# Q/K, V and FFN up projections as two 64-row array tiles, with the last FFN weights placed in dead attention weights

## The chip, the cores and the metric

The kernel runs on one core of a Trainium2 chip. The metric is the device time of one execution in microseconds (us). Executions of one kernel on one chip agree within about 0.3% of their median (seven of the kernel before: 3549.8 to 3565.8 us). Experiments 1 to 11 are one run each, and for a single run the state is listed as unknown. Each experiment was run beside the kernel before on the same chip, and that time is given with it: 3553, 3561 or 3572 us. Where runs of two chips are compared directly, a difference is uncertain by up to these 18 us.

## The reference, cut to what matters

Two layers of a recurrent attention and a SwiGLU FFN, applied one after the other to 2048 rows of width D = 576. Attention takes 64 segments of 32 rows; each has 8 memory rows in front, which are the output of the segment before, so the segments run in order.

```python
for s in range(n_seg):                      # 64 segments of 32 rows
    h = concat([mem, x[s]])                 # 40 rows x 576
    q, k, v = h @ Wq, h @ Wk, h @ Wv        # 32 heads of 128
    p = softmax(mask(q @ k.T * scale))
    o = (p @ v) @ Wo
    mem = o[:8]                             # next segment waits for this
x = x + attention(layernorm(x))
x = x + (silu(n @ w1) * (n @ w3)) @ w2      # n = layernorm(x), F = 4608
# ... and the same again (second layer, same weights)
```

## The kernel before

Layer 2 follows layer 1 by 8 segments, so there are 72 steps: 8 with layer 1 alone, 56 with both (80 columns: 2 x 40 rows), 8 with layer 2 alone. FFN work is placed between the attention stages of the steps. A scheduler orders the instructions of each engine at build time; the order then stands.

TensorE writes to 8 PSUM banks. Scores, PV and the output have four; attention's projections and the FFN share the other four in two rings:

```python
accA = Ring(banks[4:6])     # Q, K, V, transposes
accB = Ring(banks[6:8])     # FFN
...
def s_qk(gi):               # a group of 4 or 6 heads
    for kind in range(2):                       # Q, then K
        acc = accA.take()                       # one bank each
        for hl in range(hg):
            for c in range(4):                  # D = 4 x 128 + 64
                mm(accv[:, hl], lhsT=Wm[:, c, ...], rhs=ht_cols(c), ...)
            mm(accv[:, hl], lhsT=T1[...], rhs=ht_cols(tailc), ...)  # zero-padded to 128 rows
        nc.scalar.activation(QKT[...], acc[...], ACT.Copy)          # Q is copied out while K runs
def s_v(gi):                # pieces of 512 and 256 columns, one bank each
    for pi, (a0, a1) in enumerate(pieces):
        acc = accA.take()
        ...                                     # 5 matmuls
        evac("act" if pi == 0 else "dve", VG[...], acc[...])
```

576 rows of contraction make 4.5 chunks of 128; the kernel pays for 5.

## Time and profile before

| | before |
|---|---|
| median of 2 runs | 3557.41 us |
| TensorE busy | 93% |
| granted TensorE clock, mean | 0.984 |
| matmuls | 58470 |
| changes of array mode in the build order | 1437 |
| end of first step, step with both layers, tail after the last step | 79.9, 49.7 (mean), 78.3 us |

"Mode" is the shape of the array that a matmul uses: all of it, or tiles of it. The page of the profile and the timeline lines are shown in the prediction.

### The profile page before, as it was taken

To read this page: it belongs to the slowest core of one execution; us is meant where nothing else is said; L and a number is where in the kernel's file an instruction comes from. 1 tells how busy PE (TensorE), PEld (TensorE's weight loads), DVE (VectorE), ACT (ScalarE), POOL (GpSimd) and SP (SyncE) were. 2 spreads that over 40 slices of the span, in tenths; PEclk is the share of its full clock that TensorE was granted. 3 is DMA by queue.
4 is the path that set the end of the run, shared out by engine and by line. 5 is a ranking of instruction groups with operands and counts; after the bars stand their busy time and mean duration, and the time that the engine had idled before them with its cause. 6 is when DMAs were issued, how large, how long until landed. Compare 5 with 4: busy or idle time off the path is not lost.

```text
span 3562.8 us, 131473 instructions
## 1 busy us (share of the span) xinstructions
PE 3323.7 (93%) x58470; PEld 2801.4 (79%) x58470; DVE 1916.3 (54%) x5614; ACT 1621.3 (46%) x3865; POOL 61.8 (2%) x109
## 2 busy tenths in 40 slices
PE   5999999999999999999999999999999999999996
PEld 4888877877787778878787878878787878888785
DVE  3455555555555555555555555555555555555553
ACT  2544544444444444444444444444444444444441
POOL 1000000000000000000000000000000000000000
PEclk8999999999999999999999999999999999999997
DMA  8033323223222322323222322323222323223236
GB/s 256 3 95 89 102 82 95 76 73 102 74 84 69 97 87 82 89 74 96 76 82 72 101 86 82 88 74 96 77 84 73 102 77 92 83 71 96 78 114 183
DMA packets 504617, 321.65 MB, mean 90 GB/s; under 512 B 31081, under 2 KB 501361, under 8 KB 504049
## 3 DMA queue, kind: packets, MB, share of 16 engines
q1 hardware_dynamic: 500976, 306.17, 29.5%
q8 instruction: 458, 7.50, 0.9%
q0 software_dynamic: 3072, 7.08, 0.6%
q14 instruction: 111, 0.90, 0.1%
HBM read 308.42 MB, written 2.36 MB: 87 GB/s over the span
## 4 chain that ended last, share of the span: by engine, by line
PE 64%; issue 18%; DMA 8%; DVE 6%; ACT 2%; POOL 1%; SPq 0%; POOLq 0%; DVEq 0%; ACTq 0%
PE bank L174 62%; DMA W13M<-in_B_w_dram 7%; PE bank L177 2%; POOL LNS L239 1%; DVE TT L534 1%; DVE XR L491 1%; DMA T<-in_A_Wq_dram 1%; DVE LNS L233 1%; DVE LNS L234 1%; DVE HTT L535 1%; DVE XN L240 1%; DVE XR L548 0%; DVE PB L405 0%; DVE STAT L402 0%; ACT TT L533 0%
## 5 line engine op out<-in xcount | busy, mean ns | idle before, releaser
L174 PE MATMUL bank<-HT,T 128*128 128x80 bf16 x4608 | 847.0, 204 | 3.9 <-DVE HT L276 3.9
L174 PE MATMUL bank<-XTB,W13M 128*128 128x256 bf16 (+1 forms) x5184 | 695.6, 263 | 88.7 <-DMA W13M<-in_B_w_dram 80.2
L174 PE MATMUL bank<-WV,HT 128*104 128x512 bf16 (+1 forms) x2880 | 629.7, 341 | 1.7 <-ACT QKT L355 1.0
L355 ACT ACTIVATE QKT<-bank 128x480 bf16<-128x480 f32 (+1 forms) x864 | 452.2, 524 | 374.2 <-PE bank L174 325.8
L533 ACT ACTIVATE TT<-bank 128x256 bf16<-128x256 f32 (+1 forms) x648 | 233.6, 360 | 826.5 <-PE bank L174 826.3
L174 PEld LDWEIGHTS <-W13M 128*128 128x128 bf16 x5184 | 450.9, 99 | 172.7 <-DMA W13M<-in_B_w_dram 107.3
L174 PEld LDWEIGHTS <-HT 128*104 128x104 bf16 x3600 | 411.3, 128 | 191.4 <-DMA T<-in_A_Wv_dram 14.7
L174 PE MATMUL bank<-HT,WQ 128*128 128x80 bf16 x9216 | 494.5, 204 | 41.1 <-ACT HT L471 22.2
L174 PE MATMUL bank<-OT,WO 128*128 128x80 bf16 x11520 | 516.1, 202 | 12.3 <-ACT OT L429 12.1
L174 PEld LDWEIGHTS <-WO 128*128 128x128 bf16 x11520 | 473.6, 100 | 43.0 <-issue 14.2
L174 PEld LDWEIGHTS <-WQ 128*128 128x128 bf16 x9216 | 439.8, 101 | 65.5 <-issue 46.2
L174 PE MATMUL bank<-HT,WK 128*128 128x80 bf16 x9216 | 484.8, 204 | 1.4 <-DVE HT L278 1.2
L174 PEld LDWEIGHTS <-T 128*128 128x128 bf16 x4608 | 466.4, 101 | 0.6
L174 PEld LDWEIGHTS <-WK 128*128 128x128 bf16 x9216 | 437.6, 101 | 3.1 <-DVE HT L278 2.1
L534 DVE SCALAR_TENSOR_TENSOR TT<-TT,bank 128x256 bf16<-128x256 bf16 (+1 forms) x648 | 250.7, 387 | 348.3 <-ACT TT L533 346.0
L174 PE MATMUL bank<-W2C,HTT 128*128 128x288 bf16 x2284 | 349.2, 288 | 18.1 <-DVE HTT L535 10.7
L395 DVE TENSOR_TENSOR SME<-bank,maskb 104x240 f32<-104x240 f32 (+1 forms) x432 | 162.3, 376 | 351.1 <-PE bank L174 350.3
L183 DVE CAST VG<-bank 104x256 bf16<-104x256 f32 x288 | 122.1, 424 | 424.4 <-ACT VG L181 225.9
L174 PE MATMUL bank<-XTB,W13T 128*128 128x256 bf16 (+1 forms) x1296 | 338.3, 263 | 0.0
L181 ACT ACTIVATE VG<-bank 104x512 bf16<-104x512 f32 x432 | 257.7, 597 | 169.1 <-PE bank L174 160.5
L548 DVE SCALAR_TENSOR_TENSOR XR<-bank,XR 128x288 f32<-128x288 f32 x576 | 259.3, 455 | 112.1 <-PE bank L174 105.5
L174 PEld LDWEIGHTS <-HTT 128*128 128x128 bf16 x2304 | 215.0, 98 | 83.4 <-issue 20.0
(67 smaller groups left out, 3400.9 us busy)
## 6 DMA issues: line engine op xcount, KB each, us to landing
W13M<-in_B_w_dram SPq DMA_DIRECT2D x648, 256.0 KB, 3.0
W2C<-in_B_w_dram SPq DMA_DIRECT2D x319, 288.0 KB, 3.2
W13T<-in_B_w_dram SPq DMA_DIRECT2D x648, 32.0 KB, 2.6
XR<-in_A_x_dram POOLq DMA_DIRECT2D x16, 288.0 KB, 4.8
WO<-in_A_Wo_dram SPq DMA_DIRECT2D x1, 4608.0 KB, 20.6
WQ<-in_A_Wq_dram SPq DMA_DIRECT2D x4, 768.0 KB, 9.8
WK<-in_A_Wk_dram SPq DMA_DIRECT2D x4, 768.0 KB, 12.9
WV<-in_A_Wv_dram SPq DMA_DIRECT2D x4, 768.0 KB, 13.7
```

What stands on the lines that cost most here:

```text
L174: return _chain(nc.tensor.matmul(*a, **k))
L177: return _chain(nc.tensor.transpose(*a, **k))
L181: nc.scalar.activation(out_ap, in_ap, ACT.Copy)
L183: nc.vector.tensor_copy(out_ap, in_ap)
L233: nc.vector.bn_stats(st[:, 0, :], X[:, 0:288])
L234: nc.vector.bn_stats(st[:, 1, :], X[:, 288:576])
L239: nc.gpsimd.tensor_tensor(rstd, ve, mhalf[:], op=ALU.pow)
L355: nc.scalar.activation(QKT[:, qs, kind, 0:hg, :], acc[:, 0:hg * 2 * QW].rearrange("p (b n) -> p b n", b=hg), ACT.Copy)
L395: nc.vector.tensor_tensor(sme, Sps[0:104, 0:hg, :], maskb[0:104, :].unsqueeze(1).to_broadcast([104, hg, QW]), op=ALU.add)
L533: nc.scalar.activation(tt, GAv, ACT.Tanh, scale=0.5)
L534: nc.vector.scalar_tensor_tensor(tt, tt, 1.0, GAv, op0=ALU.add, op1=ALU.mult)
L548: nc.vector.scalar_tensor_tensor(Xs, yp[:, 0:288], 0.5, Xs, op0=ALU.mult, op1=ALU.add)
```

## The change

The intent: chunks of 64 rows, nine of them, two at a time side by side. Q runs on rows 0 to 63 of the array and K on rows 64 to 127; likewise the two halves of V, and w1 with w3. Nine pairs should cost 4.5 passes in place of 5. Each pair writes two PSUM banks, so a stage takes two banks at once. The other parts: matmuls of one-layer steps use only the 40 columns in use; FFN down is done per two blocks, not four; the last FFN job's weights are loaded into attention weights that are no longer needed.

```diff
-    WQ = wp.tile([P, 4, H * E], BF, name="WQ")
-    WK = wp.tile([P, 4, H * E], BF, name="WK")
...
+    WQK = wp.tile([P, NCH, H * E], BF, name="WQK")        # NCH = 9; rows 0-63 Wq, 64-127 Wk
+    WV = wp.tile([P, NCH, H * E // 2], BF, name="WV")
...
         def s_qk(gi):
-            for kind in range(2):
-                acc = accA.take()
...
+            accs = [accA.take(), accA.take()]
+            for hl in range(hg):
+                for c in range(NCH):
+                    for kind, r in ((0, 0), (1, R64)):
+                        mm(views[kind][:, hl, q0:q1], lhsT=WQK[r:r + R64, c, ...],
+                           rhs=ht_cols(r, POS[c]), ..., tile_position=(r, 0))
             for kind in range(2):
+                nc.scalar.activation(QKT[...], views[kind][:, :, q0:q1], ACT.Copy)
         def s_v(gi):
+            accs = [accA.take(), accA.take()]              # two halves of 384 or 256 columns
...
+        def up():                                           # FFN, two blocks of 128
+            if last:
+                w13, state["w2"] = tail_w[pr]               # already in WQK, WV, WO
...
+            accs = [accB.take(), accB.take()]               # gate, up
```

## The prediction

> **What bounds the kernel now.** I read the page first: busy shares, then the chain that ended last, then the groups.
>
> ```profile
> PE 3323.7 (93%) x58470; PEld 2801.4 (79%) x58470; DVE 1916.3 (54%) x5614; ACT 1621.3 (46%) x3865; POOL 61.8 (2%) x109
> ...
> PE 64%; issue 18%; DMA 8%; DVE 6%; ACT 2%; POOL 1%; SPq 0%; POOLq 0%; DVEq 0%; ACTq 0%
> PE bank L174 62%; DMA W13M<-in_B_w_dram 7%; PE bank L177 2%; POOL LNS L239 1%; DVE TT L534 1%; DVE XR L491 1%; DMA T<-in_A_Wq_dram 1%; DVE LNS L233 1%; DVE LNS L234 1%; DVE HTT L535 1%; DVE XN L240 1%; DVE XR L548 0%; DVE PB L405 0%; DVE STAT L402 0%; ACT TT L533 0%
> ...
> L174 PE MATMUL bank<-HT,T 128*128 128x80 bf16 x4608 | 847.0, 204 | 3.9 <-DVE HT L276 3.9
> L174 PE MATMUL bank<-XTB,W13M 128*128 128x256 bf16 (+1 forms) x5184 | 695.6, 263 | 88.7 <-DMA W13M<-in_B_w_dram 80.2
> ```
>
> TensorE is busy 93% of the span and holds the chain; DVE and ACT have room. A weight transfer holds 7% of the chain. But a matmul's 204 ns is latency, not what it costs in a stream. The cost is the distance from one start to the next, which the timeline shows at 1704 us (a two-layer step):
>
> ```profile
> 1704.14 0.32 PE L174 MATMUL bank<-HT,WQ 128*128 128x80 bf16 x4
> 1704.29 0.20 PE L174 MATMUL bank<-HT,T 128*128 128x80 bf16 x1
> 1704.33 0.31 PE L174 MATMUL bank<-HT,WQ 128*128 128x80 bf16 x4
> 1704.47 0.20 PE L174 MATMUL bank<-HT,T 128*128 128x80 bf16 x1
> 1704.51 0.31 PE L174 MATMUL bank<-HT,WQ 128*128 128x80 bf16 x4
> ```
>
> One head of Q is five matmuls in 0.18 us: 36 ns each for 80 columns. The same view gives 109 ns for 256 columns, 217 for 512, 122 for 288: time goes with columns, 0.417 ns each plus 2.5, and weight loads hide. With these, the before kernel's 58470 matmuls come to: Q/K 826, V 623, FFN up 631, WO 413, FFN down 282, PV 83, scores and their transposes 120, other transposes 52, together **3030 us**.
>
> Two further lines show what a change of array shape costs and what tiles side by side can do:
>
> ```profile
> 1703.49 0.27 PE L174 MATMUL bank<-XTB,W13T 128*128 128x256 bf16 x1
> 1703.69 0.23 PEld L174 LDWEIGHTS <-QKT 128*64 128x64 bf16 x11 [0.21 <-issue]
> 1703.69 0.33 PE L174 MATMUL bank<-QKT 128*64 128x40 bf16 x11
> ...
> 152.63 0.36 PE L174 MATMUL bank<-QKT 128*64 128x40 bf16 x6
> ```
>
> From the last full-array start to the first 64-column start is 0.20 us where streaming explains 0.11: some 0.09 us of drain, which recurs both ways (start distances at all changes without another wait have a median of 93 ns over the stream). The build order of the before kernel has 1437 such changes: 134 us. The other lines: 11 scores alternating between two column tiles start 14 ns apart ((0.33 - 0.19) / 10), while 6 on one tile (one layer only) start 34 ns apart ((0.36 - 0.19) / 5). So two tiles do run at once, and instructions can be issued at least every 14 ns.
>
> 3030 + 134 = 3164 of 3563 us; the remaining 400 us are waits. The step boundaries (the YTS copies) lie about 32 us apart while only one layer runs, 41 to 45 with one layer and FFN, and 50 in the 56 two-layer steps. By my count a two-layer step needs 46 us of matmuls and drains, so it waits 4.
>
> **What the Trainium skill says.** "TensorEngine Tiling (Array Packing)", Key Properties: tiles load and multiply independently, and "Changing tiling mode (not just tile) drains the TensorE". The trace agrees on both for column tiles (14 against 34 ns; 93 ns). It holds no stream of row tiles. The same page, Gotcha 1: row tiles must not write one PSUM bank at the same time; hence the change holds two banks per stage. "TensorE: Matmul & The Clock Gate", The mechanism: matmuls start strictly in order, so a run of matmuls on one tile is not paired with a later run on the other. No line here shows that for rows.
>
> **The change, part by part.**
> 1. *Fewer columns.* D = 576 is 4.5 chunks of 128, and before paid 5; nine 64-row chunks, two at once, pay 4.5. If every pair ran as one: Q/K 16128 pairs of 80 columns at 36 ns and 4608 of 40 (one-layer steps, now trimmed) at 25 = 695 us (-131); V 2592 x 162.5 + 1296 x 109 = 563 (-60); up 4536 x 109 + 1296 x 56 = 568 (-63); WO and PV trimmed in the one-layer steps, at an estimated 25 ns, -33. Sum **-287**.
> 2. *Broken pairs.* In the changed kernel's build order the scheduler does not keep pairs: runs such as 17 matmuls on rows 0-63 and then 17 on rows 64-127. Matching neighbours greedily leaves 8109 Q/K, 1266 V and 2071 up matmuls alone. Each pays a whole slot for half the work: 114 + 94 + 89 = +297; small differences in transposes add 5. So the stream comes to 3044 against 3030: **+15**. The column saving is given back.
> 3. *Drains.* Now Q/K, V and up are in 64-row mode and WO, PV and down in full mode, and the scheduler mixes them: 3145 mode changes, not 1437. At 93 ns, 292 against 134: +159. I count two thirds, because many sit where PE waits anyway (my choice): **+106**.
> 4. *Weight transfers.* Two whole up-weight slots in place of three halves let the next 256 columns load early. PE lost 80 us to W13M by the group above, part of it in the tail; I take **-60**.
> 5. *Tail.* After the last step, FFN weights stream at 185 GB/s while PE is half idle:
>
> ```profile
> 3484.00:3563.00 79.00, 47.46 (x443) 36.73 (x443) 28.66 (x98) 11.71 (x39) 1.14 (x2) 0.76 0.62 185
> ```
>
>    The last job needs 15.9 MB. Its loads can now begin once the last Q/K is done, some 17 us before the last step ends, at up to the 285 GB/s of the start: 15.9 / 285 = 56 us, plus norm and store. I take **-20**.
> 6. *Banks.* Q and K end together and both banks must be copied out (ACT, 524 ns each) before V, which takes both too. Before, one bank drained while the other filled. The two copies plus latency are about 1.3 us; PV, WO and FFN work fill much of it. 432 groups at about 0.12 us left over: **+50**. FFN down copies out twice as often (DVE 455 ns x 576 more = 262 us), merged FFN ops give some back: DVE goes to about 60%, no bound.
>
> Sum: 3557 + 15 + 106 - 60 - 20 + 50 = **3648**.
>
> **Rivals.** (a) *64-row to full is no drain.* Only the 573 changes among the other shapes then cost: 53 us against 134, two thirds of which is -54 in place of +106: 3488. For it: only column-mode changes are measured here; against it: the skill's sentence covers all modes. (b) *Row tiles do not overlap*: each matmul would pay its own slot, 41472 Q/K matmuls alone cost about 1390 us, and the kernel needs over 4500. The column tiles speak against it; I give it 2%. (c) *PSUM copies become the bound of the step*: at 0.5 us per group and stage not 0.12, 432 x 0.76 us more gives 3900+. ACT at 46% and DVE at 54% speak against; part of it may come. (d) *Everything pairs and waits were what PE lost most*: stream 2750, giving about 3300. The build order speaks against it, unless hardware pairs more than neighbours.
>
> **Range and chances.** I weigh the sum (3648) 0.5, rival (a) (3488) 0.45, and (d) 0.05: about 3559, and with a little for (c) **3570**. Each branch is uncertain by some 90 us (waits of 1.5 us a step are 84 us over 56 steps), so 8 in 10 lie in **3390 to 3710**. Over 2% faster is below 3486, over 2% slower above 3629: rival (a) splits about evenly between faster and same, the sum leans to slower. Chances **0.30 / 0.38 / 0.32**.
>
> **What would show it.** Pairing: two Q/K starts of opposite rows within 14 ns, the next pair 36 ns on. Broken pairs: runs on one tile still 36 ns apart. Drains: full to 64-row start distances 0.09 us over streaming, and PEld idle put down to issue grown well above before's 192 us. Transfers: waits for W13 nearly gone. Tail: span after the last YTS copy about 58, not 78 us. Banks: PE waiting for the Q/K and V copies, which now is under 15 us. One-layer steps should fall from 32 to about 27 us, two-layer steps stay at 48 to 52. The prediction fails low if mode changes cost nothing or pairs re-form, high if bank waits pass 0.3 us a group.

## More of the kernel before

One more stretch of the timeline of before will be compared later (columns: start, duration, engine, line, operation, operands, count). It is the end of a Q/K group and the start of V.

```profile
1705.13 0.44 ACT L355 ACTIVATE QKT<-bank 128x320 bf16<-128x320 f32 x1
...
1705.55 0.20 PE L174 MATMUL bank<-HT,T 128*128 128x80 bf16 x1
...
1705.58 0.38 PE L174 MATMUL bank<-PTS,VG 104*128 104x80 bf16 x6
...
1705.80 1.04 PE L174 MATMUL bank<-WV,HT 128*104 128x512 bf16 x4
...
1706.14 0.42 ACT L355 ACTIVATE QKT<-bank 128x320 bf16<-128x320 f32 x1
```

Q was copied out of its bank at 1705.13, while K still ran. K ends, six small PV matmuls follow, and V starts at 1705.80 in Q's old bank. K's copy comes only at 1706.14: V did not need to wait for it.

## The result, and the profile after

| | before | after |
|---|---|---|
| median of 2 runs | 3557.41 us | **4125.26 us** |
| ratio | | 1.1595 (95%: 1.1561 to 1.1628) |
| TensorE busy | 93% | 89% |
| granted clock, mean | 0.984 | 0.961 |
| matmuls; mode changes | 58470; 1437 | 86197; 3145 |
| end of first step; step with both layers; tail | 79.9; 49.7; 78.3 us | 96.5; 58.3; 79.1 us |

A ratio here is the mean time of one kernel's fast runs over that of the other's fast runs of the same rounds, so it is not quite the ratio of the medians. The changed kernel is 16% slower, far outside the predicted range of 3390 to 3710.

The page of the changed kernel (busy shares, then the chain by engine, then groups with the idle time before them and what ended most of it):

```profile
PE 3677.9 (89%) x86197; PEld 3032.9 (74%) x86197; DVE 2198.5 (53%) x5575; ACT 1473.8 (36%) x3631; POOL 63.3 (2%) x109
...
issue 55%; PE 25%; DVE 11%; ACT 4%; DMA 2%; SPq 2%; POOL 1%; DVEq 0%; POOLq 0%; ACTq 0%
...
L169 PE MATMUL bank<-WV,HT 64*104 64x384 bf16 (+1 forms) x7776 | 813.9, 325 | 114.4 <-ACT QKT L345 111.7
L169 PEld LDWEIGHTS <-HT 64*104 64x104 bf16 x7776 | 606.1, 129 | 233.2 <-issue 163.4
```

No engine became the bound: TensorE, DVE and ACT all have a smaller busy share than before. V's matmuls now have 114 us of idle time ahead of them, nearly all ended by ACT's QKT copy; before it was 1.7 us. "Issue" is time for which the profile names no releaser, drains among it. In the view of waits, weight loads (PEld) before and after:

```profile
PEld L174 <- issue: 192.4, 625, 4.1
```

```profile
PEld L169 <- issue: 628.8, 1783, 6.6
```

And the stretch of the timeline of after that answers to the one shown of before:

```profile
2010.65 0.53 PE L169 MATMUL bank<-HT,WQK 64*128 64x80 bf16 x5
...
2011.16 1.03 ACT L345 ACTIVATE QKT<-bank 128x480 bf16<-128x480 f32 x2 [3.21 <-PE bank L169]
2011.78 1.90 PE L169 MATMUL bank<-WV,HT 64*104 64x384 bf16 x9 [0.60 <-ACT QKT L345]
```

Q and K end together. ACT then copies both banks, one after the other, for 1.03 us. V stands for 0.60 us until the first copy frees a bank, and the second half of V needs the second copy. (The clock was granted at half in this stretch and in full in the one of before, so the durations of matmuls are not to be compared.)

To see where all the time went I took the start times of all TensorE matmuls from each trace, in the build order, and split each distance to the next start: column time (columns x 0.417 ns + 2.5 ns, with some slack, twice that where the clock was granted at half) is stream; at a mode change up to 0.1 us beyond it is drain; the rest is wait. The sums, in us:

| | before | after | after, four shared banks | after, emission order | after, both |
|---|---|---|---|---|---|
| stream | 3111 | 3243 | 3006 | 3046 | 2912 |
| of the stream, added by half clock | 40 | 142 | 109 | 184 | 102 |
| drain | 136 | 300 | 244 | 222 | 219 |
| wait | 301 | 566 | 321 | 1072 | 508 |
| mode changes | 1437 | 3145 | 2597 | 2335 | 2335 |
| matmuls without a neighbour on the other rows | - | 11446 | 4524 | 0 | 0 |
| clock at half (records of the trace) | 116 | 325 | 247 | 455 | 272 |

So of the 562 us that the span grew, stream is +132, drain +164 and wait +265. Half clock explains 102 of the 132: where it was granted, Q/K matmuls of 80 columns start 67 ns apart in place of 36. At full clock the stream grew by 30 only. The drain is an upper bound, because the split counts 0.1 us at a change before it counts any wait: 730 of the 3145 changes (73 us of drain) lead into a further wait of over 0.02 us, which may hide it; before, 156 of 1437 (16 us). Without these, drain grew by 106. The last three columns are experiments below.

### The profile page after: what moved, and what is told of

Same layout as the page of the kernel before. It is cut to its first block, busy times and chain, and to the rows that moved or that the text cites. A ratio compares the mean times of both kernels' runs of the same rounds, so it can differ in the third digit from the quotient of the medians.

```text
span 4124.6 us, 185858 instructions
## 1 busy us (share of the span) xinstructions
PE 3677.9 (89%) x86197; PEld 3032.9 (74%) x86197; DVE 2198.5 (53%) x5575; ACT 1473.8 (36%) x3631; POOL 63.3 (2%) x109
## 4 chain that ended last, share of the span: by engine, by line
issue 55%; PE 25%; DVE 11%; ACT 4%; DMA 2%; SPq 2%; POOL 1%; DVEq 0%; POOLq 0%; ACTq 0%
PE bank L169 25%; SPq L207 2%; DMA W<-in_B_w_dram 1%; DVE HTT L525 1%; ACT QKT L345 1%; DVE SME L372 1%; ACT SME L377 1%; DVE SME L376 1%; DVE STAT L375 1%; DVE XR L476 1%; DVE HTT L526 1%; DVE XR L539 1%; POOL LNS L232 1%; PE bank L172 1%; DVE STAT L379 1%
## 5 line engine op out<-in xcount | busy, mean ns | idle before, releaser
L169 PEld LDWEIGHTS <-WQK 64*128 64x128 bf16 x42048 | 955.0, 97 | 167.9 <-issue 133.3
L169 PE MATMUL bank<-HT,WQK 64*128 64x80 bf16 (+1 forms) x41472 | 1006.6, 196 | 69.1 <-ACT HT L455 16.4
L169 PE MATMUL bank<-WV,HT 64*104 64x384 bf16 (+1 forms) x7776 | 813.9, 325 | 114.4 <-ACT QKT L345 111.7
L169 PEld LDWEIGHTS <-HT 64*104 64x104 bf16 x7776 | 606.1, 129 | 233.2 <-issue 163.4
L169 PE MATMUL bank<-XTB,W 64*128 64x256 bf16 (+1 forms) x11016 | 750.9, 261 | 28.1 <-DVE XR L539 18.6
L169 PEld LDWEIGHTS <-W 64*128 64x128 bf16 x11016 | 561.4, 94 | 125.7 <-issue 32.1
L178 DVE CAST VG<-bank 104x384 bf16<-104x384 f32 (+1 forms) x432 | 221.0, 512 | 743.1 <-PE bank L169 731.5
L169 PE MATMUL bank<-OT,WO 128*128 128x80 bf16 (+1 forms) x11520 | 538.6, 197 | 27.3 <-ACT OT L406 22.1
L539 DVE SCALAR_TENSOR_TENSOR XR<-bank,XR 128x288 f32<-128x288 f32 x1152 | 498.1, 453 | 119.5 <-PE bank L169 89.7
L169 PE MATMUL bank<-W2C,HTT 128*128 128x288 bf16 x2232 | 433.9, 287 | 80.2 <-DVE HTT L525 36.0
L345 ACT ACTIVATE QKT<-bank 128x480 bf16<-128x480 f32 (+3 forms) x864 | 374.7, 482 | 284.8 <-PE bank L169 279.6
```

The costliest lines, as they stand in the source:

```text
L169: return _chain(nc.tensor.matmul(*a, **k))
L178: nc.vector.tensor_copy(out_ap, in_ap)
L345: nc.scalar.activation(QKT[:, qs, kind, 0:hg, q0:q1], views[kind][:, :, q0:q1], ACT.Copy)
L539: nc.vector.scalar_tensor_tensor(Xs, yp[:, 0:288], 0.5, Xs, op0=ALU.mult, op1=ALU.add)
```

## The experiments

**Theory**: the stage that holds both of accA's banks is the root. V needs two banks, and its halves can run side by side only once both are copied out. TensorE waits, and the scheduler, which estimates when banks come free, breaks the pairs (one half starts in the bank that is free first) and puts other modes' work between. **Rivals**: the mode changes alone; the broken pairs alone; row tiles that overlap poorly.

One number is used throughout: the distance from the last Q/K start of a group to the next V start, and the column time of other matmuls placed in it. What is left over is uncovered; it holds the waits and the drains of this stretch (after: about 0.56 and 0.18 us; after with four shared banks: 0.05 and 0.14).

| mean over about 430 to 450 groups, us | other work | distance | uncovered |
|---|---|---|---|
| before | 0.50 | 0.57 | 0.07 |
| after | 0.73 | 1.43 | 0.70 |
| before, holding two banks | 0.68 | 1.06 | 0.38 |
| after, emission order | 0.51 | 1.36 | 0.85 |
| after, four shared banks | 0.48 | 0.66 | 0.18 |

**1. What a change between the full array and 64 rows costs.** The tail matmul of V in the kernel before has zeros in half its rows; here it is issued on the other 64 alone.

```diff
-                    mm(acc[0:104, 0:a1 - a0], lhsT=HTt[:, 4, :], rhs=T2[:, a0:a1], start=False, stop=True)
+                    mm(acc[0:104, 0:a1 - a0], lhsT=HTt[0:64, 4, :], rhs=T2[0:64, a0:a1], start=False, stop=True,
+                       tile_position=(0, 0))
```

> The kernel before, with only the fifth matmul of each V piece issued on 64 rows (the zero half of its operands left out); nothing else is changed, and its build order differs in 61 places of 58470. Mode changes go from 1437 to 2809, 1372 more. If a change between the full array and 64 rows drains as the column-mode changes of before do (about 96 ns): +132 us, some 3690. If it is no drain (rival a of the prediction): 3557 within 0.5%.

Measured: 3708.34 against 3571.94, +136 us for 1372 more changes, 99 ns each. The timeline of this run shows single ones:

```profile
1812.29 1.04 PE L174 MATMUL bank<-WV,HT 128*104 128x512 bf16 x4
1813.26 0.42 PE L174 MATMUL bank<-T,HT 64*104 64x512 bf16 x1
1813.69 0.60 PE L174 MATMUL bank<-WV,HT 128*104 128x256 bf16 x4
1814.21 0.31 PE L174 MATMUL bank<-T,HT 64*104 64x256 bf16 x1
```

From 1813.69, four matmuls of 256 columns should take 0.44 us; the 64-row one starts after 0.52. The way back (1813.26 to 1813.69, one matmul of 512 columns at 0.217) costs 0.21 more here; in 422 of 430 such places of this trace it is 0.13. Rival (a) of the prediction, that these changes are free, falls. At 99 ns, the 1708 changes that the change added are worth at most 170 us; how much of that is hidden in waits no run shows.

**2. Holding two banks, with nothing else of the change.** In the kernel before, Q and K are interleaved by head and both copied at the end; the V pieces likewise. Full array throughout.

```diff
-            for kind in range(2):
-                acc = accA.take()
+            accs = [accA.take(), accA.take()]
+            for hl in range(hg):
+                for kind in range(2):
...
+            for kind in range(2):
+                acc = accs[kind]
                 nc.scalar.activation(QKT[:, qs, kind, 0:hg, :], ...)
```

> The kernel before, all on the full array, but Q and K of a group are interleaved by head and both PSUM banks are held until both are done, and the two V pieces likewise, as the changed kernel holds them. Mode changes 1326, not more than before. If holding both banks is a main cause: waits for the QKT and VG copies rise by over 100 us, time 3650 to 3800. If the mode changes and broken pairs are the cause and banks are covered by other work: under 3600.

Measured: 3719.31 against 3571.94, +147 us, with fewer mode changes than before (1326) and 720 more matmuls, since V of a four-head group is split in two here. Uncovered time per group went from 0.07 to 0.38 us; 0.31 x 432 is 134 of the 147 us. By the split, wait rose by 151, stream by 13, and drain fell by 10. Holding two banks costs time without any row tile.

**3. The pairs kept together.** The changed kernel with TensorE in emission order.

```diff
-    FORCE_PE_ORDER=False,
+    FORCE_PE_ORDER=True,
```

> The changed kernel with all TensorE instructions kept in the order in which the program emits them: all 30456 pairs stand side by side (24733 with 5670 or more matmuls left single in the changed kernel, 11446 single in all), and mode changes fall from 3145 to 2335. If broken pairs and mode mixing are the main cause: minus about 250 us of stream and 78 us of drains, some 3800. If the reordering mostly used time in which TensorE would have waited for a bank anyway: 4100 or above, with waits for the copies up by what the stream lost.

Measured: 4358.36 against 3571.94 of before. All pairs stand, stream falls by 197 us and drain by 78, as hoped; waits rise by 506. So the broken pairs and mixed modes are not the root: the scheduler spent them to fill time in which TensorE would have waited for banks, and it gained by that.

**4. Four banks for attention and FFN together.** The only edit is the ring:

```diff
-    accB = Ring(banks[6:8])
+    accA.slots = list(banks[4:8])
+    accB = accA
```

> The changed kernel with one ring of four PSUM banks for attention and FFN in place of two rings of two, so that Q/K and V need not wait for each other's copies unless FFN took the banks between. In its build order mode changes fall to 2597, single matmuls from 11446 to 4524. If bank holding is the root (it breaks pairs and makes the scheduler mix modes): 3700 to 3850. If row tiles simply overlap poorly: within 2% of 4125.

Measured: **3588.85** against 3571.94, below the range that was expected if banks were the root. Of the 16%, all but 0.5% is gone by that one edit: 536 us. (Before gains by the same edit too; see the control.) Stream fell by 237, drain by 56, wait by 245. The timeline of this run at a Q/K group's end:

```profile
1809.42 0.85 PE L170 MATMUL bank<-HT,WQK 64*128 64x80 bf16 x38
...
1810.20 0.39 PE L170 MATMUL bank<-PTS,VG 104*128 104x80 bf16 x6
1810.36 1.03 ACT L346 ACTIVATE QKT<-bank 128x480 bf16<-128x480 f32 x2 [0.91 <-PE bank L170]
...
1810.52 1.62 PE L170 MATMUL bank<-WV,HT 64*104 64x384 bf16 x14
```

ACT copies for 1.03 us as before, but V starts 0.16 us after the copies begin, in two other banks.

**5. The control: the same ring in the kernel before.**

```diff
-    accB = Ring(banks[6:8])
+    accA.slots = list(banks[4:8])
+    accB = accA
```

> The kernel before with the one ring of four PSUM banks, as the control of the changed kernel's run with it. If the shared ring took 536 us off the changed kernel because only that one holds two banks per stage, before gains little: 3480 to 3560, from waits of 100 us at most for banks and from 1240 mode changes in place of 1437 (19 us). If four shared banks are simply better for any such kernel: under 3350.

Measured: 3474.56 against 3553.45, -79 us (2.2%), 5 us below the expected range. The ring helps before too: its uncovered time per group does not move (0.07), but its waits shrink by 64 us in all, some 20 each at FFN down and at Q/K. So 457 of the 536 us belong to what the change did with the banks. With four shared banks in both kernels, the change still costs 114 us (about 96 when each is taken against before on its own chip), although it contains the trimming of one-layer steps, which experiment 10 finds worth 80.

**6. Emission order with four banks.** The edits of experiments 3 and 4 together.

```diff
-    FORCE_PE_ORDER=False,
+    FORCE_PE_ORDER=True,
...
-    accB = Ring(banks[6:8])
+    accA.slots = list(banks[4:8])
+    accB = accA
```

> The changed kernel with the shared ring of four banks and with TensorE kept in emission order: all pairs side by side, 2335 mode changes (2597 without the pin). With two rings of two banks the pin cost 233 us (4358 against 4125). If that was banks alone, it now costs under 100 us or even gains: 3500 to 3690. If the scheduler's filling of other waits (softmax, FFN) is what counts: 3750 or more.

Measured: 3657.05 against 3553.45. The pin costs 68 us in place of 233. Against experiment 3 this is also the cleanest test of the banks: the 86197 matmuls run in the same order, with the same pairs and the same 2335 changes, and only the ring differs. It takes 701 us off (4358 to 3657), 564 of them wait. TensorE's wait for the Q/K copies, in experiment 3 and here (total, times, longest):

```profile
PE bank L169 <- ACT QKT L345: 257.0, 367, 2.7
```

```profile
PE bank L170 <- ACT QKT L346: 32.4, 26, 2.9
```

The stream, all in pairs, is 2912 us. At full clock, two Q/K starts of opposite rows are most often 3 or 4 ns apart, and a pair of 80 columns takes 36 ns (median), just what one full-array matmul took; pairs of 256 and 384 columns take 109 and 163. Row tiles overlap fully. But waits, for which no filling is left, are 187 us above those of the free order.

**7. A faster copy, which was not faster.** DVE copies K's bank while ACT copies Q's.

```diff
-                nc.scalar.activation(QKT[:, qs, kind, 0:hg, q0:q1], views[kind][:, :, q0:q1], ACT.Copy)
+                evac("act" if kind == 0 else "dve", QKT[:, qs, kind, 0:hg, q0:q1], views[kind][:, :, q0:q1])
```

> The changed kernel with K's bank copied out by DVE while ACT copies Q's, so that both banks of accA come free some 0.5 us earlier in each of 432 groups; 3145 mode changes as before, single V matmuls 787 in place of 1266. If the time until both banks are copied is what V waits for: 0.2 to 0.5 us a group, 90 to 210 us less, 3915 to 4035. If the waits have another cause, or DVE's queue is no faster: 4080 or more.

Measured: 4270.97 against 3561.34 of before; 146 us slower than the changed kernel, where I had expected 90 to 210 faster. In the trace the first copy ends 0.64 us after the last Q/K matmul in both kernels (medians), but the second ends 1.49 us after it on the mean, not 1.16. That DVE was still in other work then is the likely reason, and not shown. From first to last start, V takes 1.83 us in place of 1.57 on the mean. By the split, wait rises by 95 us (by 107 ahead of V) and half clock adds 67 (489 us granted at half, not 327), while the stream is otherwise 19 shorter. My expectation of the sign was wrong, because I took DVE for free at 53% busy. The later bank fits the theory, but nearly half of the loss is clock.

**8. Attention and FFN apart.** The FFN as before (full array, one bank a block, no tail load), attention in row tiles on two banks.

```diff
-            accs = [accB.take(), accB.take()]
+                acc = accB.take()
...
-                        mm(v[:, fb, lo:hi], lhsT=w13[r:r + R64, c, ...], rhs=XTB[r:r + R64, POS[c], lo:hi], ...,
-                           tile_position=(r, 0))
+                        mm(accv[:, gu, lo:hi], lhsT=W13M[:, wss[gu], c, ...], rhs=XTB[:, c, lo:hi], ...)
```

> The changed kernel with the FFN as in the kernel before (full array, one bank a block, four blocks to a down step, no tail load); attention still in row tiles on two banks. To compare with the changed kernel without tail load (4144). If the loss lies in the attention's banks: 3950 or more. If the FFN's two-bank units and their mode changes (3159 to 2675, 48 us) carry as much: 3750 to 3850.

Measured: 3963.77, as expected if most of the loss lies in attention's banks. Against the changed kernel without tail load (next), 180 us go with the FFN's part of the change; the other 402 us over before (3561.34 on this chip) remain with attention's part alone.

**9. Without the tail load.**

```diff
-        last = 4 * j + 4 >= NSEG + LAG
+        last = False
```

> The changed kernel with the last job's FFN weights loaded through the rings as in all other jobs. The tail after the last YTS copy is 79 us in both kernels. If loading into the dead attention weights gained what the slower landing in 64 partitions costs: tail above 85 us and time above 4130. If it gave nothing: 4125 within 10 us.

Measured: 4144.12 (before on this chip: 3553.45), against 4125.26: the tail load is worth 19 us. The tail after the last step is 101.8 us without it and 79.1 with it; before it was 78.3, and 80.2 in experiment 8, with the FFN of before. So it only wins back what the new FFN lost. The issue view points to one likely reason: before, an up transfer of 128 partitions, and after, one of 64 partitions (columns: size, median us from issue to landing). Half clock and other differences of the two FFNs were not separated from it.

```profile
W13M<-in_B_w_dram SPq DMA_DIRECT2D x648, 256.0 KB, 3.0
```

```profile
W<-in_B_w_dram SPq DMA_DIRECT2D x612, 288.0 KB, 4.8
```

And the tail of after, in the same columns as the prediction's line for before (busy times, then clock, DMA share and GB/s at the end): 154 GB/s, where before reached 185.

```profile
4045.50:4124.60 79.10, 66.56 (x730) 56.78 (x730) 33.33 (x80) 8.76 (x21) 1.14 (x2) 0.65 0.74 154
```

**10. Trimmed one-layer steps and four banks, full array.** Of the change, only the 40-column matmuls in one-layer steps are put into the kernel before, with the shared ring.

```diff
+        q0, q1 = layers[0] * QW, (layers[-1] + 1) * QW
...
-                mm(PVv[:, hl, :], ..., rhs=PTS[0:104, ss, hl, :],
+                mm(PVv[:, hl, q0:q1], ..., rhs=PTS[0:104, ss, hl, q0:q1],
```

Q/K, WO and the copies after them are cut to q0:q1 in the same way.

> The kernel before with the shared ring and with the changed kernel's trimming of the one-layer steps (Q/K, PV and WO on 40 columns where only one layer runs), the full array everywhere. Trimming takes 5120 Q/K and 2560 WO and 512 PV matmuls from 36 to about 25 ns: 90 us off the run with the shared ring alone, if those steps are bound by TensorE; 40 us or less if their copies and softmax bind them.

Measured: 3394.48 against 3553.45, 80 us below the run with the ring alone. One-layer steps without FFN fall from 32 to 27 us. The trimming was a good part of the change, and needs no row tiles.

**11. Row tiles in attention where banks are not the bound.** Experiment 8 with the shared ring.

```diff
-    accB = Ring(banks[6:8])
+    accA.slots = list(banks[4:8])
+    accB = accA
```

> The same with the shared ring of four banks: Q/K and V in row tiles, FFN on the full array, 2123 mode changes. Against the kernel before with the shared ring and the trimming (3394, full array everywhere) this shows what row tiles in attention are worth when banks are not the bound: 871 more mode changes at 99 ns are +86 us, the Q/K and V columns saved at most -190 us, slower first step +17. Expected if mode changes eat the saving: 3400 to 3500. If pairing gives what the columns promise: 3250 to 3330.

Measured: 3521.75 (before on this chip: 3561.34). Against 3394 with the full array, the same ring and the same trimming, row tiles in attention *cost* 127 us, more than expected. By the split of start distances, the stream is 29 us shorter (Q/K 766 against 791, V 624 against 641), drain 82 longer (871 more changes), waits 74 longer (30 of them TensorE's wait for W13M, 110.8 against 80.5). The first step takes 95.2 against 73.2 us; from 20 to 80 us weights arrive at 216 to 267 GB/s, those of Q/K and V into 64 partitions at a time; in experiment 10 they arrive at 333 to 356 GB/s from 20 to 60 us. Half-clock time is 237 us against 109, which adds 58 to the stream. At full clock the pairs thus saved 87 us, and the visits to their mode cost 82: about even. The loss is the clock and the waits.

**12. A version that beats both.** To experiment 10 a fourth up-weight slot was added (the deeper prefetch of the change), with the FFN product in place to make room.

```diff
-    N_W13 = 3
+    N_W13 = 4
...
-                tt = TT[:, 0, fb, lo:hi]
+                tt = HTT[:, hs, fbi, lo:hi]
```

> The kernel before with shared ring, trimmed one-layer steps, a fourth up-weight slot (so a whole next pair of up weights can load early, as in the changed kernel) and the FFN product in place to make room. TensorE's waits at up matmuls (97 us in the run without the fourth slot, mostly for W13M) should fall by 50 to 80 us: 3310 to 3345. If these waits are the tail's transfer rate alone: 3385 or more.

Measured in 3 rounds: **3319.19** (3317.68 to 3319.62, 4 runs) against 3561.34; ratio 0.9328 (95%: 0.931 to 0.9346). That is 75 us below experiment 10, where this wait was still 80.5 us. The wait of TensorE for this transfer, before and in this version (total, times, longest):

```profile
PE bank L174 <- DMA W13M<-in_B_w_dram: 80.2, 97, 2.7
```

```profile
PE bank L174 <- DMA W13M<-in_B_w_dram: 23.2, 26, 2.4
```

What stays open: the clock. The trace's records grant half clock for 116 us before and 325 us after. Of the 48 pieces of after, 44 last 3.4 or 6.8 us, half of all within 4 us of a step boundary, and two last 51 us each, in the first step and in the tail. At half speed that is at most about 105 us of the loss. It went down with the waits in experiment 4, but row-tile kernels stay at twice the time of the others even with four banks (237 and 247 against 109). In experiment 2, waits of the full array rose by 151 us and half clock only from 116 to 128, which speaks against the waits alone. What brings it on was not separated.

## Why the prediction was wrong

Point by point, in the prediction's own order.

1. *Fewer columns, and broken pairs (+15 together).* The count of broken pairs was right and so was the warning that the build order gives the saving back. Measured stream is +132, but +30 at full clock; the other 102 are half clock, for which the prediction had no term. With whole pairs and four banks it is -199, or -261 at full clock, where -287 was hoped for: the 36 ns a pair was right. One sum is small: 114 us for the broken Q/K pairs fits singles of 40 columns at 19 ns; the trace has them at 25, which gives 131.
2. *Drains (+106).* The mechanism and the 93 ns were right: 99 measured for this kind of change. The factor of two thirds was a guess, and stays untested: drain rose by 164 if all of it is counted and by 106 without the changes that lead into a wait. That the second number is the predicted one may be luck.
3. *Weight transfers (-60).* Right: TensorE's waits for up weights fell from 80 to 10 us in the view of waits.
4. *Tail (-20).* Wrong: 0. The load starts early, and gains 19 us against the same kernel without it, but the new FFN had made the tail 23 us longer.
5. *Banks (+50).* **This is the step that failed.** The prediction put it as "432 groups at about 0.12 us left over". Measured, 0.70 us is left over after Q/K, against 0.07 before: 0.63 x 432 = 272 us at this stage alone. Wait is 245 of that (1 before); part of the rest are drains, which point 2 counts too. The text had the mechanism ("Q and K end together and both banks must be copied out"), and the 1.3 us that the two copies take, but took for granted that other work fills nearly all of it. The build order, which I had read for pairs and mode changes, also showed what stands there: 0.73 us of other work on the mean, in more than eight of ten groups under 0.7 us. Subtracting that from 1.3 would have given about 0.6.
6. *The parts as a sum.* Banks, pairs and mode changes were added as if independent. Experiments 3 and 4 show that they are one cause: given four banks, the same scheduler breaks less than half as many pairs and changes mode 548 times less. Four shared banks took 536 us off the changed kernel and 79 off before, so 457 of the loss of 568 hang on two banks.

Of the rivals, (c), that copies out of PSUM bound the step at 0.5 us a group, was the true one, and its 3900 was nearest; it was set aside because ACT stood at 46% and DVE at 54%. Mean busy shares say nothing on it: what counts is the time from the end of a stage to its copied bank. (a) fell by experiment 1, (b) by pairs that start 3 or 4 ns apart and take 36 ns, (d) by the result. One-layer steps were said to fall to 27 us; they rose to 35 to 40; with four banks they were 29 to 30 (experiment 4) and, on the full array, 27 (experiment 10).

## What to carry to other kernels

Count, for each stage, the banks it holds at once against the banks it may take, and read in the build order how much other work stands between its end and the next stage that needs them; compare that with the time of the copies, not with the copying engine's busy share. Two tiles that run side by side also finish side by side, so they need twice the banks to keep copy and compute apart. And count every change of array mode as a cost (99 ns here): splitting work into tiles pays only where a visit to the mode saves clearly more than the drains around it (in experiment 11, 87 us of columns against 82 of drains).

## What the Trainium skill lacked or had wrong

- "TensorEngine Tiling (Array Packing)", Key Properties: it says that a change of tiling mode drains, and gives no cost. Here it was 99 ns for each change between full array and 64 rows (1372 more changes, 136 us), and a median of 93 ns between full array and column tiles.
- The same page, Gotcha 1 (PSUM Pressure) and PSUM Bottleneck: it says that row tiles write different banks and that copying out of PSUM may become the bottleneck. It lacks how to count: a stage holds two banks until both are copied out, which left 0.70 us a group uncovered with two banks in the ring and 0.18 with four, while the copying engines stood at 36% and 53%.
- "TensorE: Matmul & The Clock Gate", Measured speedup vs the span model: it gives about 4 ns from tile to tile for packs. The trace agrees (3 or 4 ns, most often). No row there covers a stream of pairs on 64-row tiles with fresh weights for each: here a pair took what one full-array matmul takes, 36 ns for 80 columns, 109 for 256 and 163 for 384.
- "DMA: Bandwidth & Descriptors", Rules for kernel authors: it advises one 128-partition transfer over two to partition halves, as they serialize. The runs are in line with this and add a size: 288 KB into 64 partitions landed in 4.8 us (each beside its partner for the other half), 256 KB into 128 in 3.0. Whether the halves are the reason was not separated.
